# Weight conversions of the expert stage: all low parts on VectorE, weights in the long unit's first product, w-pieces in the second products

## The chip, the cores and the metric

The kernel runs on one core of a Trainium2 chip. The metric is the device time of one launch in microseconds (us). TensorE's clock has two levels, 1.2 and 2.4 GHz; the profile shows the granted clock of a stretch as a share of full speed.

## What is computed

Local attention over chunks feeds a mixture of eight experts (two per token), and that feeds a dense block with a maximum over three products. All of it is float32. The expert stage, where the change lies, is the middle function:

```python
def _moe_ref(x, w_gate, w_noise, noise, w1, w2):      # x 3072x512, w1 8x512x1024, w2 8x1024x512
    ...
    top2 = np.argpartition(-noisy_logits, 2, axis=1)[:, :2]
    ...
    for e in range(E):
        for k in range(2):
            mask = top2[:, k] == e
            h = np.maximum(x[mask] @ w1[e], 0.0)
            out[mask] += top2_w[mask, k, None] * (h @ w2[e])

def _moe2_ref(x, w1, w2, w3, w_out):                   # w1, w2, w3 512x768, w_out 768x512
    h = np.maximum(np.maximum(x @ w1, x @ w2), x @ w3)
    return h @ w_out
```

## The kernel before

**Precision.** A float32 product is made of three matrix products of a reduced type (`three`): high x high, high x low, low x high. So each operand is kept in two tiles, `hi` and `lo`. `split` makes them: ScalarE copies the source into `hi` (a cast), and then another engine subtracts, `lo = src - hi`. That engine is GpSimd (the page's POOL) unless the caller names VectorE (DVE).

**Expert stage.** It runs in 16 units, two per expert: an even, long unit (four token tiles of 128, 512 rows; unit 0 has 384) and an odd, short one (320 rows: two tiles and 64; unit 1 has 448). `unit(u)` has two parts. The **first product** has 8 steps; each makes 12 matmuls into one of two PSUM banks, `sc` and `pp` in turn, then ScalarE's relu writes `h[:, 0]` (L788) and VectorE writes the low part `h[:, 1]` from the same bank (L792). TensorE may overwrite a bank two steps later, after both have read it. The **second product** has 8 steps for each token tile (steps 8 to 39 in a long unit, 8 to 31 in a short one), sums into one of three banks (`misc`, `tabp`, `po`), and `put` copies each finished tile out, in turn by ScalarE (L656) and VectorE (L658). `unit_turn` transposes a token tile of the next unit and splits it into `xT`, its low part on VectorE, four times per second product (the last at step 28 of a long unit).

**Side tasks.** Two kinds of work are hung on the steps by a table, `planned(u)`: at each step the tasks are issued behind the relu and the low part of that step. The program's order is the code's order, on every engine, and each engine runs its own instructions in that order.

- A **weight tile**: 128x1024 floats of w1 or w2 (eight per expert). `wload` loads it on SyncE's queue into one of three staging buffers `st`; `wsplit` casts it on ScalarE (L195), subtracts on GpSimd (L196), then loads the part that stands three places further on. There are 12 tile slots.
- A **w-piece**: 24 parts of the later dense block's weights, which arrive as 64-bit numbers. `narrow` makes float32 of one in five VectorE instructions (L241 to L245) behind a square on ScalarE, and adds on GpSimd (L246). For the 18 pieces of the first three weight matrices `sums` forms four differences on VectorE (L204) and `cast` splits the eight blocks, with ScalarE (L195) and GpSimd (L196), and stores both parts to DRAM (`m2s`). The other six are only stored (`m2f`).

In the table of before, a long unit of experts 1 to 6 has four pieces, at steps 1, 4, 12 and 26 (`sums` at 3, 6, 20, 34 and `cast` at 4, 7, 22, 36), and six weight tiles at 0, 3, 9, 16, 24 and 32; a short unit has two weight tiles, at 9 and 14. The six pieces that are only stored come last, in units 10 and 12. So units 2, 4, 6, 8 and 10 have differences and casts in their first product, and units 2, 4, 6 and 8 have them at the end of the second one.

**Dense block.** Block 0 (`second`, four token tiles) makes 18 products of 12 matmuls, the calls of `step(s)` standing ahead of product s. In it the rows of block 1 are gathered (`block_fetch`, GpSimd's queue), weighted (`block_mix`, L690 and L691 on VectorE) at even s and transposed (`block_turn`, L703 on TensorE) at odd s.

Of the kernel before, what the change touches and what calls it, by code (L numbers as in the profile page):

```python
# [8 lines left out]
F32 = mybir.dt.float32  # L9
F32R = mybir.dt.float32r  # L10
# [40 lines left out]
def tile_kernel(ctx, tc, qT, kT, mkT, vw, wgn, noise, w1, w2, m2w, out):  # L51
# [103 lines left out]
    turns = [("f64", j, h) for j in range(12) for h in range(2)]  # L155
    wparts, plan = list(range(8)), []

    def planned(u):

        e = u // 2  # L160
        if u == 0:
            return [(8 + k, None) for k in range(4)]
        if u % 2:
            return [(8 * e + 12 + k, 9 + 5 * k) for k in range(2)]
        c = [(turns.pop(0), *at) for at in ((1, 3, 4), (4, 6, 7), (12, 20, 22), (26, 34, 36)) if turns]
        w = [(8 * e + 6, 0), (8 * e + 7, 3), (8 * e + 8, 9), (8 * e + 9, 16), (8 * e + 10, 24), (8 * e + 11, 32)]
        return sorted(c + w, key=lambda x: x[1])

    for u in range(2 * E):
        plan.append([x for x in planned(u) if not isinstance(x[0], int) or x[0] < 8 * E])  # L170
        wparts += [x[0] for x in plan[u]]
# [28 lines left out]
    def sums():  # L200

        for v, j, h in formed[-1:]:
            for o, l, r, op in ((0, 7, 6, ALU.add), (1, 0, 4, ALU.subtract), (2, 4, 7, ALU.subtract), (3, 5, 1, ALU.subtract)):
                DVE.tensor_tensor(v[:, o, :], v[:, l, :], v[:, r, :], op=op)  # L204

    def cast():

        while formed:
            v, j, h = formed.pop()
            top = made["cv"].tile([128, 8, 128], F32R, name="top", bufs=1)  # L210
            split(v, top, v.bitcast(F32R))
            for r, t in enumerate((top, v)):
                SP.dma_start(m2s[j, :, :, h, r, :].rearrange("o p n -> p o n"), t if r else t.bitcast(F32))

    def wsplit(eng=None):
        n = wnext[1]
        if n == len(wparts):
            return
        wnext[1] += 1
        st = wst.pop(n)  # L220
        if isinstance(wparts[n], int):
            w = wtile(wparts[n])
            split(st, w[:, 0, :], w[:, 1, :], eng)
        else:
            _, j, h = wparts[n]
            val = narrow(st.rearrange("p (n t) -> p n t", t=2))
            if j < 9:
                formed.append((val, j, h))
            else:
                SP.dma_start(m2f[j - 9, :, 512 * h:512 * h + 512], val[:, 4:8, :].rearrange("p i n -> p (i n)"))  # L230
        wload()

    def narrow(st):
# [6 lines left out]
        ACT.activation(sq, top.bitcast(F32), AF.Square)  # L240
        DVE.tensor_scalar(val, top, 5, 2, op0=ALU.logical_shift_left, op1=ALU.logical_shift_right)  # L241
        DVE.scalar_tensor_tensor(val, top, -(1 << 30), val, op0=ALU.bitwise_and, op1=ALU.bitwise_or)
        DVE.scalar_tensor_tensor(v, sq, 2.0 ** -30, v, op0=ALU.is_ge, op1=ALU.mult)
        DVE.tensor_scalar(top, val, -(1 << 23), None, op0=ALU.bitwise_and)
        DVE.scalar_tensor_tensor(sq, low.bitcast(U32), 2.0 ** -52, top.bitcast(F32), op0=ALU.mult, op1=ALU.mult)  # L245
        POOL.tensor_tensor(v, v, sq, op=ALU.add)  # L246
        return full
# [518 lines left out]

    def unit(u):
# [5 lines left out]
        else:  # L773
            side = [[] for _ in range(steps)]
            for _, *at in plan[u]:
                for i, task in zip(at, (wsplit, sums, cast)):
                    side[i].append(task)
# [77 lines left out]
    def second(xT, dst, step=lambda s: None, along=[]):  # L855
# [275 lines left out]
```

## Time and profile before

| | |
|---|---|
| median of 3 runs | 1181.28 us (1180.49 to 1181.43) |
| profiled execution, its own time | 1179.27 us |
| its span | 1177.5 us |
| TensorE matmuls (PE) busy | 1121.1 us, 95% of the span |
| VectorE (DVE) busy | 592.2 us, 50% |
| GpSimd (POOL) busy | 416.1 us, 35% |
| ScalarE (ACT) busy | 390.2 us, 33% |

The busy time of one engine is an average over stages with different limits, and a busy TensorE is not TensorE at its peak. The stages are better read by stretches: how long a unit takes, and at which granted clock. The units' borders are the starts of their first matmuls into `sc` in the timeline.

### The profile page before, as it was taken

To read this page: it belongs to the slowest core of one execution; us is meant where nothing else is said; L and a number is where in the kernel's file an instruction comes from. 1 tells how busy PE (TensorE), PEld (TensorE's weight loads), DVE (VectorE), ACT (ScalarE), POOL (GpSimd) and SP (SyncE) were. 2 spreads that over 40 slices of the span, in tenths; PEclk is the share of its full clock that TensorE was granted. 3 is DMA by queue.
4 is the path that set the end of the run, shared out by engine and by line. 5 is a ranking of instruction groups with operands and counts; after the bars stand their busy time and mean duration, and the time that the engine had idled before them with its cause. 6 is when DMAs were issued, how large, how long until landed. Compare 5 with 4: busy or idle time off the path is not lost. (4 is left out here: it accounts for less than half of the span.)

```text
span 1177.5 us, 17436 instructions
## 1 busy us (share of the span) xinstructions
PE 1121.1 (95%) x6804; PEld 935.5 (79%) x6804; DVE 592.2 (50%) x1164; ACT 390.2 (33%) x680; POOL 416.1 (35%) x331
## 2 busy tenths in 40 slices
PE   8887999999999999999999999999999999999997
PEld 5777878878788778788788898887787778787886
DVE  4587862463563662572633422135566675655221
ACT  5877422332332332333323322222321143113110
POOL 3001021355354363463444432133266524543000
PEclk9999799999999999999999999999999999999999
DMA  8999551365465374473553546257466744766501
GB/s 239 309 292 287 164 170 34 120 195 170 146 191 190 114 222 141 130 237 112 161 180 125 154 160 188 72 153 227 141 185 217 230 129 134 223 188 214 179 1 39
DMA packets 113690, 199.07 MB, mean 169 GB/s; under 512 B 8576, under 2 KB 46592, under 8 KB 113600
## 3 DMA queue, kind: packets, MB, share of 16 engines
q1 hardware_dynamic: 76736, 109.86, 29.8%
q0 software_dynamic: 34272, 78.13, 21.5%
q10 hardware_dynamic: 2592, 9.88, 2.6%
q8 instruction: 56, 0.92, 0.3%
q14 instruction: 34, 0.28, 0.1%
HBM read 151.18 MB, written 46.66 MB: 168 GB/s over the span
## 5 line engine op out<-in xcount | busy, mean ns | idle before, releaser
L93 PE MATMUL pp<-xT,w 128*128 128x512 f32 (+3 forms) x912 | 199.6, 369 | 12.9 <-DVE h L792 12.9
L93 PE MATMUL sc<-xT,w 128*128 128x512 f32 (+3 forms) x912 | 195.0, 361 | 8.7 <-DVE h L792 7.3
L93 PEld LDWEIGHTS pp<-xT,w 128*128 128x128 f32 x912 | 163.9, 196 | 36.4 <-DVE h L792 15.4
L93 PEld LDWEIGHTS sc<-xT,w 128*128 128x128 f32 x912 | 158.2, 190 | 33.7 <-ACT h L788 8.2
L196 POOL TENSOR_TENSOR w<-st,w 128x1024 fp32r<-128x1024 f32 x52 | 126.9, 2442 | 149.1 <-ACT w L195 149.1
L93 PE MATMUL po<-w,h 128*128 128x512 f32 x548 | 135.1, 395 | 0.0
L93 PE MATMUL misc<-w,h 128*128 128x512 f32 x522 | 127.8, 394 | 0.0
L93 PE MATMUL tabp<-w,h 128*128 128x512 f32 x498 | 121.5, 394 | 0.0
L93 PEld LDWEIGHTS po<-w,h 128*128 128x128 f32 x548 | 101.0, 188 | 20.6
L93 PEld LDWEIGHTS misc<-w,h 128*128 128x128 f32 x522 | 96.5, 188 | 19.8
L93 PEld LDWEIGHTS tabp<-w,h 128*128 128x128 f32 x498 | 92.2, 188 | 19.0
L252 POOL DMA_INDIRECT g<-xd,tok x56 | 53.2, 949 | 107.8 <-DVE count_i L535 50.0
L792 DVE SCALAR_TENSOR_TENSOR h<-sc,h 128x256 fp32r<-128x256 f32 (+2 forms) x96 | 39.7, 442 | 84.9 <-ACT h L788 84.9
L792 DVE SCALAR_TENSOR_TENSOR h<-pp,h 128x256 fp32r<-128x256 f32 (+2 forms) x96 | 39.8, 443 | 82.6 <-ACT h L788 82.6
L252 POOL DMA_INDIRECT g<-ys,rows x48 | 49.7, 1035 | 87.4 <-DMA ys<-y 46.1
L195 ACT CAST w<-st 128x1024 fp32r<-128x1024 f32 x75 | 78.3, 1046 | 3.2 <-DVE st L896 2.8
L788 ACT ACTIVATE h<-sc 128x512 fp32r<-128x512 f32 (+3 forms) x64 | 33.1, 517 | 111.5 <-PE sc L93 111.5
L788 ACT ACTIVATE h<-pp 128x512 fp32r<-128x512 f32 (+3 forms) x64 | 33.1, 517 | 108.8 <-PE pp L93 108.8
L196 POOL TENSOR_TENSOR val<-val,top 128x1024 fp32r<-128x1024 f32 x18 | 45.5, 2527 | 52.9 <-ACT top L195 52.9
L196 DVE TENSOR_TENSOR xT<-xp,xT 128x512 fp32r<-128x512 f32 (+1 forms) x35 | 23.4, 668 | 66.2 <-ACT xT L195 66.2
L246 POOL TENSOR_TENSOR val<-val,sq 128x512 f32<-128x512 f32 x24 | 30.9, 1287 | 65.4 <-DVE sq L245 62.2
L196 DVE TENSOR_TENSOR xT<-idle,xT 128x512 fp32r<-128x512 f32 (+1 forms) x29 | 18.7, 645 | 61.8 <-ACT xT L195 61.8
(196 smaller groups left out, 1649.4 us busy)
## 6 DMA issues: line engine op xcount, KB each, us to landing
st<-in_w SPq DMA_DIRECT2D x64, 512.0 KB, 3.6
w<-m2s POOLq DMA_DIRECT2D x27, 1024.0 KB, 9.1
ys<-y SPq DMA_DIRECT2D x48, 256.0 KB, 3.9
st<-in_m2w SPq DMA_DIRECT2D x24, 512.0 KB, 3.8
m2s<-top SPq DMA_DIRECT2D x18, 512.0 KB, 3.6
m2s<-val SPq DMA_DIRECT2D x18, 512.0 KB, 3.2
xT<-m2s POOLq DMA_DIRECT2D x9, 1024.0 KB, 5.9
w<-m2s POOLq DMA_DIRECT2D x9, 768.0 KB, 7.2
```

Source lines behind the costliest of these rows:

```text
L93: PE.matmul(o, l, r, start=start, stop=stop)
L195: ACT.copy(hi, src)
L196: (eng or POOL).tensor_tensor(lo, src, hi.bitcast(F32), op=ALU.subtract)
L246: POOL.tensor_tensor(v, v, sq, op=ALU.add)
L252: POOL.indirect_dma_start(out=g[0:n], out_offset=None, in_=src, in_offset=bass.IndirectOffsetOnAxis(ap=idx, axis=0))
L788: ACT.activation(h[:, 0, 0:n], p[:, 0:n], AF.Relu)
L792: DVE.scalar_tensor_tensor(o[:, c], p[:, c], 0.0, h[:, 0, c].bitcast(F32), op0=ALU.max, op1=ALU.subtract)
```

## The change

The table becomes another one. All eight weight tiles of a long unit (its own w2 and the next expert's w1) stand in its first product, the cast of tile k at step k and its subtraction at step k+1. Short units have none. A piece is cut in five tasks (`one` to `five`) at steps i, i+2, i+4, i+5 and i+6: i is 9 in a short unit, 9, 18 and 27 in the long units of experts 2, 4 and 6 (units 4, 8, 12), and 9 and 22 in the other long ones. The six pieces that are only stored come first. All subtractions and additions of both kinds go to VectorE; GpSimd keeps its DMA issues in this stage. The loads move with the tasks: after the subtraction of a weight tile, after `two` of a piece.

In block 0, transposes and gathers move from ahead of a product into its middle (`middle`, behind six of its 12 matmuls), and the last transpose one step later into the second product.

```diff
-    turns = [("f64", j, h) for j in range(12) for h in range(2)]
+    turns = [("f64", j, h) for j in (9, 10, 11, *range(9)) for h in range(2)]
...
         if u == 0:
-            return [(8 + k, None) for k in range(4)]
-        if u % 2:
-            return [(8 * e + 12 + k, 9 + 5 * k) for k in range(2)]
-        c = [(turns.pop(0), *at) for at in ((1, 3, 4), (4, 6, 7), (12, 20, 22), (26, 34, 36)) if turns]
-        w = [(8 * e + 6, 0), (8 * e + 7, 3), (8 * e + 8, 9), (8 * e + 9, 16), (8 * e + 10, 24), (8 * e + 11, 32)]
-        return sorted(c + w, key=lambda x: x[1])
+            return [(8 + k,) for k in range(4)]
+        w = [] if u % 2 else [(8 * e + 4 + k, k, k + 1) for k in range(8) if 8 * e + 4 + k < 8 * E]
+        at = [9] if u % 2 else [9, 18, 27] if e % 2 == 0 else [9, 22]
+        return w + [(turns.pop(0), i, i + 2, i + 4, i + 5, i + 6) for i in at if turns]
...
+            def low(eng):
+                (eng or POOL).tensor_tensor(w[:, 1, :], st, w[:, 0, :].bitcast(F32), op=ALU.subtract)
+                wload()
+
+            return [n, lambda eng: ACT.copy(w[:, 0, :], st), low]
...
-        POOL.tensor_tensor(v, v, sq, op=ALU.add)
-        return full
...
+        def one(eng):
+            ACT.activation(sq, top.bitcast(F32), AF.Square)
+            DVE.tensor_scalar(val, top, 5, 2, op0=ALU.logical_shift_left, op1=ALU.logical_shift_right)
+            DVE.scalar_tensor_tensor(val, top, -(1 << 30), val, op0=ALU.bitwise_and, op1=ALU.bitwise_or)
+
+        def two(eng):
+            DVE.scalar_tensor_tensor(v, sq, 2.0 ** -30, v, op0=ALU.is_ge, op1=ALU.mult)
+            DVE.tensor_scalar(top, val, -(1 << 23), None, op0=ALU.bitwise_and)
+            DVE.scalar_tensor_tensor(sq, low.bitcast(U32), 2.0 ** -52, top.bitcast(F32), op0=ALU.mult, op1=ALU.mult)
+            wload()
+
+        def three(eng):
+            DVE.tensor_tensor(v, v, sq, op=ALU.add)
+            if j >= 9:
+                SP.dma_start(m2f[j - 9, :, 512 * h:512 * h + 512], v)
+                return
+            for o, l, r, op in ((0, 7, 6, ALU.add), (1, 0, 4, ALU.subtract), (2, 4, 7, ALU.subtract), (3, 5, 1, ALU.subtract)):
+                DVE.tensor_tensor(full[:, o, :], full[:, l, :], full[:, r, :], op=op)
+
+        def four(eng):
+            if j < 9:
+                hi.append(made["cv"].tile([128, 8, 128], F32R, name="top", bufs=1))
+                ACT.copy(hi[0], full)
+
+        def five(eng):
+            if j < 9:
+                DVE.tensor_tensor(full.bitcast(F32R), full, hi[0].bitcast(F32), op=ALU.subtract)
+                for r, t in enumerate((hi[0].bitcast(F32), full)):
+                    SP.dma_start(m2s[j, :, :, h, r, :].rearrange("o p n -> p o n"), t)
...
                     for k in range(4):
+                        if k == 2:
+                            middle(6 * f + 2 * w + r)
...
-        side[3].insert(0, partial(step, 19))
+        side[4].insert(0, partial(middle, 19))
...
-            if s % 2 and s >= 5:
-                block_turn(b + 1, s // 2 - 2)
-                block_fetch(b + 1, s // 2)
...
+        def middle(s):
+            if s % 2 and s >= 5:
+                block_turn(b + 1, s // 2 - 2)
+                block_fetch(b + 1, s // 2)
```

Three places show what stands in a row now. The first is VectorE in the first product of unit 8 (a long unit); `h_2064` and those that follow are the eight `h` tiles, `val`, `sq` and `st` belong to the pieces, `w` is a weight tile. Before:

```order
L792 SCALAR_TENSOR_TENSOR h_2064<-sc,h_2064 128x512
L792 SCALAR_TENSOR_TENSOR h_2065<-pp,h_2065 128x512
L241 TENSOR_SCALAR val<-st 128x512
L242 SCALAR_TENSOR_TENSOR val<-st,val 128x512
L243 SCALAR_TENSOR_TENSOR val<-sq,val 128x512
L244 TENSOR_SCALAR st<-val 128x512
L245 SCALAR_TENSOR_TENSOR sq<-st 128x512
L792 SCALAR_TENSOR_TENSOR h_2066<-sc,h_2066 128x512
L792 SCALAR_TENSOR_TENSOR h_2067<-pp,h_2067 128x512
L204 TENSOR_TENSOR val<-val 128x128 x4
L792 SCALAR_TENSOR_TENSOR h_2068<-sc,h_2068 128x512
```

The same place now:

```order
L811 SCALAR_TENSOR_TENSOR h_2064<-sc,h_2064 128x512
L811 SCALAR_TENSOR_TENSOR h_2065<-pp,h_2065 128x512
L213 TENSOR_TENSOR w_122<-st,w_122 128x1024
L811 SCALAR_TENSOR_TENSOR h_2066<-sc,h_2066 128x512
L213 TENSOR_TENSOR w_123<-st,w_123 128x1024
L811 SCALAR_TENSOR_TENSOR h_2067<-pp,h_2067 128x512
L213 TENSOR_TENSOR w_124<-st,w_124 128x1024
L811 SCALAR_TENSOR_TENSOR h_2068<-sc,h_2068 128x512
```

The groups of four and five instructions between two `h` are gone; one weight subtraction stands in each gap instead.

The second place is VectorE at the end of unit 8, from its last piece to the first `h` of unit 9. Before:

```order
L241 TENSOR_SCALAR val<-st 128x512
L242 SCALAR_TENSOR_TENSOR val<-st,val 128x512
L243 SCALAR_TENSOR_TENSOR val<-sq,val 128x512
L244 TENSOR_SCALAR st<-val 128x512
L245 SCALAR_TENSOR_TENSOR sq<-st 128x512
L196 TENSOR_TENSOR xT_2063<-xp,xT_2063 128x4x64
L204 TENSOR_TENSOR val<-val 128x128 x4
L658 COPY y<-tabp 128x512
L792 SCALAR_TENSOR_TENSOR h_2064<-sc,h_2064 128x256
```

Now:

```order
L231 TENSOR_SCALAR val<-st 128x512
L232 SCALAR_TENSOR_TENSOR val<-st,val 128x512
L194 TENSOR_TENSOR xT_2063<-xp,xT_2063 128x4x64
L235 SCALAR_TENSOR_TENSOR val<-sq,val 128x512
L236 TENSOR_SCALAR st<-val 128x512
L237 SCALAR_TENSOR_TENSOR sq<-st 128x512
L241 TENSOR_TENSOR val<-val,sq 128x512
L246 TENSOR_TENSOR val<-val 128x128 x4
L255 TENSOR_TENSOR val<-val,top 128x1024
L670 COPY y<-tabp 128x512
L811 SCALAR_TENSOR_TENSOR h_2064<-sc,h_2064 128x256
```

The addition (L241) and the piece's subtraction (L255) have come to VectorE, ahead of the copy of `y` and the next unit's first `h`.

The third place is TensorE in block 0, at two of its products; `xp` is the bank of the transposes. Before:

```order
L93 MATMUL sc<-xT_130,w_6646 128x512 x12
L703 MATMUL xp<-ident,g 128x128 x4
L93 MATMUL pp<-xT_130,w_6646 128x512 x12
L93 MATMUL idle<-xT_130,w_6722 128x512 x12
L703 MATMUL xp<-ident,g 128x128 x4
```

Now:

```order
L93 MATMUL sc<-xT_130,w_6646 128x512 x12
L93 MATMUL pp<-xT_130,w_6646 128x512 x6
L715 MATMUL xp<-ident,g 128x128 x4
L93 MATMUL pp<-xT_130,w_6646 128x512 x6
L93 MATMUL idle<-xT_130,w_6722 128x512 x12
L93 MATMUL sc<-xT_130,w_6722 128x512 x6
L715 MATMUL xp<-ident,g 128x128 x4
```

The four transposes stand half a product further on.

## Rows read from the trace of the kernel before

**Rows 1.** Windows: stretch, length, engines' busy us (instructions), granted clock, DMA share, GB/s.
```profile
217.70:267.20 49.50, 46.88 (x205) 37.83 (x204) 32.94 (x46) 18.84 (x27) 25.31 (x13) 0.97 0.51 156
267.20:301.40 34.20, 32.39 (x178) 29.13 (x176) 11.06 (x26) 9.15 (x16) 16.12 (x11) 0.95 0.58 183
301.40:351.60 50.20, 47.32 (x205) 37.95 (x205) 33.31 (x46) 18.86 (x27) 25.30 (x13) 0.97 0.51 155
351.60:384.20 32.60, 30.82 (x177) 27.54 (x177) 11.00 (x26) 9.15 (x16) 16.12 (x11) 1.00 0.58 190
...
632.20:678.00 45.80, 45.57 (x206) 36.91 (x206) 20.44 (x34) 16.12 (x24) 19.95 (x11) 1.00 0.44 133
678.00:708.50 30.50, 30.50 (x177) 27.51 (x176) 7.99 (x22) 8.32 (x15) 10.87 (x9) 1.00 0.44 155
```

**Rows 2.** Timeline, unit 2's first product: start us, us, engine, instruction [idle <- releaser].
```profile
234.54 2.69 POOL L196 TENSOR_TENSOR val<-val,top 128x1024 fp32r<-128x1024 f32 x1 [1.57 <-ACT top L195]
235.09 2.70 DVE L243 SCALAR_TENSOR_TENSOR val<-sq,val 128x512 f32<-128x512 f32 x1
239.63 4.38 PE L93 MATMUL pp<-xT,w 128*128 128x512 f32 x12 [2.62 <-DVE h L792]
```

**Rows 3.** Timeline, start of unit 3.
```profile
267.22 3.22 DVE L204 TENSOR_TENSOR val<-val 128x128 f32<-128x128 f32 x4 [1.06 <-POOL val L246]
270.60 1.04 ACT L195 CAST top<-val 128x1024 fp32r<-128x1024 f32 x1 [7.08 <-DVE val L204]
272.71 3.02 PE L93 MATMUL sc<-xT,w 128*128 128x320 f32 x12 [1.81 <-DVE h L792]
```

**Rows 4.** Timeline, first product of unit 14 (no wait in it).
```profile
717.21 2.88 PE L93 MATMUL pp<-xT,w 128*128 128x512 f32 x12
717.47 0.60 ACT L788 ACTIVATE h<-sc 128x512 fp32r<-128x512 f32 x1 [2.12 <-PE sc L93]
718.10 0.69 DVE L792 SCALAR_TENSOR_TENSOR h<-sc,h 128x512 fp32r<-128x512 f32 x1 [2.02 <-ACT h L788]
719.93 2.88 PE L93 MATMUL sc<-xT,w 128*128 128x512 f32 x12
```

**Rows 5.** Instructions of tile w on VectorE: ns min/median/max, first and last start.
```profile
L196 DVE TENSOR_TENSOR w<-st,w x23: 1210/1224/2231, 112.7 to 982.1; 128x1024 fp32r<-128x1024 f32 x23
```

**Rows 6.** Loads into st, units 2 to 14: us from issue to landing.
```profile
DMA to landing us min/median/max: 3.5/3.8/4.9
```

**Rows 7.** Timeline, VectorE in a piece of unit 2: its first, last instruction, its differences.
```profile
224.66 0.42 DVE L241 TENSOR_SCALAR val<-st 128x512 int32<-128x512 int32 x1
...
227.17 0.69 DVE L245 SCALAR_TENSOR_TENSOR sq<-st 128x512 f32<-128x512 uint32 x1
...
240.36 1.02 DVE L204 TENSOR_TENSOR val<-val 128x128 f32<-128x128 f32 x4 [0.19 <-POOL val L246]
```

**Rows 8.** Line 243, all 24 executions: ns min/median/max, first and last start.
```profile
L243 DVE SCALAR_TENSOR_TENSOR val<-sq,val x24: 691/693/2700, 225.9 to 671.7; 128x512 f32<-128x512 f32 x24
```

**Rows 9.** Timeline, second product of unit 12 and first steps of unit 13.
```profile
654.61 3.56 PE L93 MATMUL misc<-w,h 128*128 128x512 f32 x15
...
677.98 1.92 PE L93 MATMUL sc<-xT,w 128*128 128x320 f32 x12
678.18 0.69 DVE L658 COPY y<-misc 128x512 f32<-128x512 f32 x1 [4.24 <-PE misc L93]
...
680.46 0.56 DVE L792 SCALAR_TENSOR_TENSOR h<-sc,h 128x256 fp32r<-128x256 f32 x2 [1.59 <-ACT h L788]
...
681.49 0.75 PE L93 MATMUL sc<-xT,w 128*128 128x320 f32 x4
```

**Rows 10.** The page's costliest groups: busy us, mean ns | idle before, releaser.
```profile
L196 DVE TENSOR_TENSOR xT<-xp,xT 128x512 fp32r<-128x512 f32 (+1 forms) x35 | 23.4, 668 | 66.2 <-ACT xT L195 66.2
```

**Rows 11.** Waits of TensorE in block 0: us in total, times, longest.
```profile
PE xp L703 <- DVE g L691: 2.2, 2, 1.4
PE xp L703 <- ACT h L870: 0.7, 1, 0.7
```

More of the change, by code (lines that the diff above doesn't have):

```diff
@@ L161, in planned @@
         if u == 0:
-            return [(8 + k, None) for k in range(4)]
-        if u % 2:
-            return [(8 * e + 12 + k, 9 + 5 * k) for k in range(2)]
-        c = [(turns.pop(0), *at) for at in ((1, 3, 4), (4, 6, 7), (12, 20, 22), (26, 34, 36)) if turns]
-        w = [(8 * e + 6, 0), (8 * e + 7, 3), (8 * e + 8, 9), (8 * e + 9, 16), (8 * e + 10, 24), (8 * e + 11, 32)]
-        return sorted(c + w, key=lambda x: x[1])
+            return [(8 + k,) for k in range(4)]
+        w = [] if u % 2 else [(8 * e + 4 + k, k, k + 1) for k in range(8) if 8 * e + 4 + k < 8 * E]
+        at = [9] if u % 2 else [9, 18, 27] if e % 2 == 0 else [9, 22]
+        return w + [(turns.pop(0), i, i + 2, i + 4, i + 5, i + 6) for i in at if turns]
     for u in range(2 * E):
-        plan.append([x for x in planned(u) if not isinstance(x[0], int) or x[0] < 8 * E])
+        plan.append(planned(u))
         wparts += [x[0] for x in plan[u]]
@@ L198, in tile_kernel, with wtasks @@
     formed = []
[L200 to L213, printed above, removed]
     def wsplit(eng=None):
+        for task in wtasks()[1:]:
+            task(eng)
+    def wtasks():
         n = wnext[1]
         if n == len(wparts):
-            return
+            return [n]
         wnext[1] += 1
@@ L222, in wsplit, with narrow @@
             w = wtile(wparts[n])
[L223 to L233, printed above, removed]
+            def low(eng):
+                (eng or POOL).tensor_tensor(w[:, 1, :], st, w[:, 0, :].bitcast(F32), op=ALU.subtract)
+                wload()
+            return [n, lambda eng: ACT.copy(w[:, 0, :], st), low]
+        _, j, h = wparts[n]
+        return [n] + narrow(st.rearrange("p (n t) -> p n t", t=2), j, h)
+    def narrow(st, j, h):
         top, low = st[:, :, 1], st[:, :, 0]
@@ L239, in narrow @@
         sq = made["cv"].tile([128, 512], F32, name="sq", bufs=1)
[L240 to L245, printed above, removed]
-        POOL.tensor_tensor(v, v, sq, op=ALU.add)
-        return full
+        hi = []
+        def one(eng):
[23 more added lines that the diff above has]
+                    SP.dma_start(m2s[j, :, :, h, r, :].rearrange("o p n -> p o n"), t)
+        return [one, two, three, four, five]
     def fetch(src, idx, n):
@@ L765, in ahead, with task_of @@
                     task(0, j)
+    def task_of(part, now, i):
+        if i == 0:
+            now += wtasks()
+            assert wparts[now.pop(0)] == part
+        now[i](DVE)
     def unit(u):
@@ L774, in unit @@
             side = [[] for _ in range(steps)]
-            for _, *at in plan[u]:
-                for i, task in zip(at, (wsplit, sums, cast)):
-                    side[i].append(task)
+            for part, *at in plan[u]:
+                now = []
+                for i, t in enumerate(at):
+                    side[t].append(partial(task_of, part, now, i))
         for f in range(8):
@@ L853, in out_part, with second @@
         three(o, h, w, i == 0, i == 5)
-    def second(xT, dst, step=lambda s: None, along=[]):
+    def second(xT, dst, step=lambda s: None, middle=lambda s: None, along=[]):
         h = [big.tile([128, 2, 512], F32R, name=f"h{i}") for i in range(6)]
@@ L1024, in block @@
                     block_fetch(1, j)
-            second(xTs["b", b] if b else xts[0], dst, step, along)
+            second(xTs["b", b] if b else xts[0], dst, step, middle, along)
     for b in range(len(blocks)):
```

## The prediction

> **What bounds the kernel now.** I read the windows first, one for each unit of the expert stage. Unit 12, a long one, takes 45.8 us and unit 13, a short one, 30.5, both at a granted clock of 1.00 and with matmuls over practically the whole window. Unit 2 takes 49.5 and unit 4 50.2; units 6, 8 and 10 are like unit 4 (50.2 to 50.3). Unit 3 takes 34.2 at a clock of 0.95 and unit 5 32.6 at 1.00; unit 7 is like unit 3, unit 9 like unit 5 [rows 1]. The same matmuls run in all long units from unit 2 on, and the same in all short ones from unit 3 on, so nine units lose 2 to 4.5 us each and the rest of the stage loses next to nothing. TensorE is the bound, and those losses are what a side engine can give back.
>
> Then the timeline, inside such a unit. In unit 2 the low part of an `h`, on VectorE, comes late, TensorE waits 2.62 us for its bank, and the 12 matmuls behind the wait take 4.38 us [rows 2] where an undisturbed product starts the next one 2.72 later (719.93 - 717.21) [rows 4]: they run in part at the lower clock, 1.2 GHz instead of 2.4. Why is the low part late? Five instructions of a piece stand ahead of it, and one, L243, takes 2.70 us beside a GpSimd subtraction of 2.69 us that began just earlier [rows 2]; its usual time is 0.69 [rows 8]. At the start of unit 3 it goes through ScalarE: its cast of `top` waited for four differences that took 3.22 us, and the relu stands behind that cast; TensorE waits 1.81 us [rows 3]. Last I looked at block 0, where TensorE waits 2.9 us for transposes' operands and their bank [rows 11].
>
> **The change part by part.**
>
> *Removed: the piece work between two `h` of a long unit's first product, and casts of pieces at the end of its second product's GpSimd chain.* If the nine units fall to the undisturbed length, the long ones give 49.5 + 4 x 50.2 - 5 x 45.8 = 21.3 us, and the short ones 2 x 34.2 + 2 x 32.6 - 4 x 30.5 = 11.6 us [rows 1]. Together 32.9; the cost of the lower clock is in these lengths and isn't added again.
>
> *Added in the first product: eight subtractions and eight casts of weight tiles.* One subtraction on VectorE is 1.22 us [rows 5], one `h` 0.69 [rows 4], so 1.91 us of the 2.72 of a step. Does it delay an `h`? Product sc ends when pp begins, at 717.21; relu runs from 717.47, `h` from 718.10 to 718.79, and its bank is wanted at 719.93 [rows 4], 1.1 us later. The next `h` can start 2.72 us after this one; the subtraction between them ends 1.91 after it. So no wait. ScalarE has 0.60 + about 1.05 (the cast of the same size in [rows 3]) of 2.72. I cost this part at nothing, under the cover of TensorE's own step, and that cover has an end: see the loads below.
>
> *Added in second products: pieces, wholly on VectorE.* A piece's first five instructions take 227.17 + 0.69 - 224.66 = 3.20 us; the addition 0.69 (by the row of the same size in [rows 8]) and the differences 1.02 [rows 7] make 1.76 with a hand-over; ScalarE's cast 1.04 [rows 3] and two hand-overs 1.15; the last subtraction 1.22 [rows 5], 1.27 with one. This is one chain of 7.4 us, since each task needs the one before it and VectorE runs in order. In a short unit it is one chain, in a long one with two it ends long before the unit. Units 8 and 12 have three full ones (unit 4 has two of the short, stored kind). From the start of the second product: the last `h` is done at about 1.6, two weight subtractions bring 4.0, three chains 26.2, three `xT` low parts on the way (0.67 each [rows 10], the last a half tile) 28.0, the copy of `y` 0.69 [rows 9] 28.7, the next unit's first `h` 0.56 [rows 9] 29.2. TensorE wants that bank at 681.49 - 654.61 = 26.9 [rows 9]. So the `h` is late by 2.4 us in units 9 and 13. The other end: with the bare durations (2.92 for the five, 0.4 less over each chain) it is late by 1.2. I take 2.4, since the 3.20 is a measured sequence. Of the short units' waits of about 1.8 us two of four came with the lower clock, at 1.6 us more (34.2 against 32.6) [rows 1]; half of that on each makes 3.2. Two units: **6.4 us** lost, between 2.4 and 8.0.
>
> With two full pieces the same count is 4.0 + 14.8 + 1.8 + 0.7 (the copy that no longer falls into a gap) = 21.3, then the `y` copy at the unit's end and `h` behind its relu, before 26.9: nothing lost.
>
> *GpSimd* loses its arithmetic in the stage. What it keeps (gathers and the loads of `m2s`) can issue earlier, and nobody waits for it: the units without a wait had the same gathers. I cost it at nothing either way. SyncE's queue carries the same loads and stores in another order; behind a load that waits for a subtraction stand the stores of `y`, which have three buffers.
>
> At this point a rule bears on which durations hold. L243 took 2.70 us beside GpSimd and 0.69 else [rows 2, 8]. The Trainium skill, SBUF — State Buffer, section "Who interferes with whom", says that VectorE and GpSimd share one pair of ports as an exclusive lock, and that a VectorE instruction with two SBUF inputs is blocked for the whole of a GpSimd instruction that reads SBUF. The trace agrees: 2.70 is the 0.69 and the rest of the 2.69. By that rule the short durations hold once GpSimd does no arithmetic there; without it, the second rival's time would stand.
>
> *Block 0.* Half a product is 1.36 us, so the waits of 1.4 and 0.7 us ahead of transposes vanish; the last transpose moves three matmuls, 0.68, against 0.7. Of 2.9 us [rows 11] I take **2.8**; at the least 2, if what is late moves along.
>
> **Sum.** 1179.27 (profiled execution: span 1177.5 and 1.77 around it) - 32.9 - 2.8 + 6.4 = 1150.0. The profiled execution is 2.0 below the median of the runs, so the median to expect is **1152.0**, 2.5% faster.
>
> **The rivals.**
>
> 1. *No tail.* VectorE ends its three chains in time, because the hand-overs are hidden or the first piece starts before the last weight tile's step. For it: the 1.2 us of the lower end need little more to vanish. Against: the order puts the pieces behind both subtractions and ahead of the next `h`. 1179.27 - 32.9 - 2.8 + 2.0 = 1145.6.
>
> 2. *Stretched pieces.* VectorE's instructions are long for another reason than GpSimd, and L243's 2.70 or the differences' 3.22 come back: about 2.2 us more in each chain. With two pieces the tail ends 21.3 + 4.4 + 0.7 + 0.6 = 27.0 against 26.9, just on time; with three, 6.6 us later still. 1152.0 + 2 x 6.6 = 1165. For it: the maxima in rows 5 and 8. Against: each that I looked at lay beside a GpSimd instruction.
>
> 3. *Loads set the pace, slower than before.* There are three staging buffers. The load of tile k+3 starts when the subtraction of tile k is done; its landing, cast (1.05), the relu behind it (0.6), the `h` (0.69 and a hand-over) and the subtraction (1.22) make landing + 3.6 us for three steps of 2.72. At the median landing of 3.8 us [rows 6] that is 7.4 of 8.2 us; 4.6 us is where it begins to bind, and the 1.1 us of slack of a bank hold it to about 5.7. Loads are denser now: eight behind one first product instead of four. If they took 8 us, the cast in front of a relu would be 3.5 us late by the sixth tile and 7 by the eighth, less the slack 5.9, with 1.6 for the clock 7.5 in each of the six units with eight tiles: 45 us on the 1145.6, 1190. It outweighs the gain from a landing of about 7.3 us on. Against: 4.9 is the longest seen.
>
> 4. *The wait only changes its place.* The late `h` comes from something beside the pieces and stays: 1181. Against: units 12 and 13, with the same `h` and no differences, lose nothing.
>
> **How the numbers follow.** The forecast has 0.56 (1147 to 1157 by the bounds of the tails), no tail 0.24, stretched pieces or tails in more units 0.13, slow loads 0.04, no change of use 0.03. The range 1144 to 1161 holds the first two and part of the third. A measurement of this kernel can tell some 0.2% (2.4 us) from no change. Slower by more: 0.04, the loads. Within it: 0.03. Faster: 0.93.
>
> **What would show it.** Right: units 2, 4, 6, 8 and 10 at 45 to 46 us and units 3, 5 and 7 at 30.5, at a clock of 1.00; in units 9 and 13 one wait of TensorE for `h`, near their third product, of 1 to 3 us; L235, the old L243, never above 0.75 us; the weight subtraction near 1.22 in all units; no ScalarE wait for `st` above 2 us; block 0 some 3 us shorter. Wrong: ScalarE's casts of `w` waiting for DMA in long units (the third rival), a wait for `h` in the first product of a long unit, or piece chains well above 7.4 us.

## The result and the profile after

The changed kernel takes 1148.47 us (median of 4 runs, 1147.20 to 1151.13), the kernel before 1181.36 beside it: a ratio of 0.9725 with an interval of 0.9704 to 0.9745. The profiled execution took 1149.49 us, with a span of 1147.7. So the change makes the kernel 2.75% faster; 1152.0 was predicted, with a range of 1144 to 1161, so the time lies inside it, 3.5 us under the forecast.

The windows of the changed kernel, in the columns of [rows 1]: units 4 and 5, unit 9, unit 13, unit 14, and block 0.

```profile
295.00:340.70 45.70, 45.47 (x206) 37.10 (x206) 30.77 (x45) 18.89 (x26) 3.27 (x4) 1.00 0.58 186
340.70:371.20 30.50, 30.50 (x177) 27.51 (x176) 13.57 (x33) 7.83 (x15) 3.27 (x4) 1.00 0.42 126
493.20:525.20 32.00, 30.80 (x178) 27.57 (x176) 15.76 (x39) 8.78 (x16) 3.32 (x4) 1.00 0.53 152
647.10:679.30 32.20, 30.82 (x177) 27.55 (x177) 15.96 (x39) 8.79 (x16) 5.04 (x6) 1.00 0.49 150
679.30:726.50 47.20, 45.80 (x206) 37.05 (x206) 24.35 (x39) 15.33 (x23) 0.81 (x2) 1.00 0.72 223
757.50:822.00 64.50, 64.49 (x300) 53.04 (x299) 33.59 (x45) 19.75 (x29) 24.48 (x24) 1.00 0.59 176
```

Unit 4 was 50.2 us at a clock of 0.97 and unit 5 was 32.6 [rows 1]; they are 45.7 and 30.5 now, with matmuls over the whole window and a clock of 1.00. Units 2 to 8 and 10 are all like this (45.2 to 45.7 and 30.5 to 30.6). GpSimd is busy for 3.3 us in unit 4 instead of 25.3; over the whole span it falls from 416.1 to 215.9 us, and VectorE, which took the arithmetic over, only rises from 592.2 to 632.7. Three units are longer than their kind: 9 and 13 (32.0 and 32.2 where 30.5 is undisturbed), and 14 (47.2 where it took 45.7 before).

All waits of TensorE for `h` between unit 2 and the end of unit 15 are one group of the waits (us in total, times, longest):

```profile
PE sc L93 <- DVE h L811: 3.8, 3, 1.4
```

In the kernel before, nine units had one each, of 2.62 us in [rows 2] and 1.81 in [rows 3]. The three that are left are the three long windows above. Line 243 is now L235, and its durations in all 24 executions, with those of the weight subtraction, can be set beside [rows 8] and [rows 5] (ns, min/median/max):

```profile
L235 DVE SCALAR_TENSOR_TENSOR val<-sq,val x24: 681/682/694, 199.9 to 715.6; 128x512 f32<-128x512 f32 x24
...
L213 DVE TENSOR_TENSOR w<-st,w x67: 1212/1215/1241, 114.7 to 782.0; 128x1024 fp32r<-128x1024 f32 x67
```

The longest of line 243 was 2700 ns; the longest L235 is 694. No weight subtraction by L213 is above 1241 ns. The 2231 of [rows 5] is no counterpart: it ran in the dense block (857.38 us), where subtractions of this size still take up to 2586 ns in the changed kernel.

Stage by stage, predicted and measured:

| stage | predicted, us | measured, us |
|---|---|---|
| units 2 to 10, without the wait in unit 9 | -32.9 | 351.7 - 1.4 - 383.9 = -33.6 |
| late `h` in units 9 and 13 | +6.4 | 1.4 + 1.7 = +3.1 |
| unit 14 | 0 | 47.2 - 45.7 = +1.5 |
| from the end of unit 15 to the start of the last block | -2.8 | 317.5 - 320.6 = -3.1 |
| ahead of unit 2, and the last stretch | 0 | +1.5 and +1.0 |
| sum | -29.3 | -29.6 |

The two spans differ by 29.8; the 0.2 that is left is 0.1 in each of units 11 and 12, the precision of the windows. The change hardly touches the two stretches of the line before the sum (it puts one piece into unit 1, which takes 41.4 us in both kernels): the stage ahead of unit 0 took 132.8 us before and 134.0 after, and between 130.2 and 137.2 in the profiled executions of this study. So the length of a unit is a sharper measure than a median here.

### The profile page after: what moved, and what is told of

Read it like the earlier page. It is cut to its first block, busy times and chain, and to the rows that moved or that the text cites. A ratio compares the mean times of both kernels' runs of the same rounds, so it can differ in the third digit from the quotient of the medians.

```text
span 1147.7 us, 17323 instructions
## 1 busy us (share of the span) xinstructions
PE 1106.3 (96%) x6803; PEld 927.2 (81%) x6804; DVE 632.7 (55%) x1258; ACT 391.6 (34%) x680; POOL 215.9 (19%) x237
## 5 line engine op out<-in xcount | busy, mean ns | idle before, releaser
L93 PE MATMUL pp<-xT,w 128*128 128x512 f32 (+3 forms) x912 | 190.5, 356 | 0.0
L93 PEld LDWEIGHTS pp<-xT,w 128*128 128x128 f32 x912 | 157.4, 188 | 19.5 <-DVE h L811 0.2
L213 DVE TENSOR_TENSOR w<-st,w 128x1024 fp32r<-128x1024 f32 x67 | 81.0, 1217 | 11.2 <-ACT w L216 11.0
L216 ACT CAST w<-st 128x1024 fp32r<-128x1024 f32 x67 | 70.1, 1046 | 4.4 <-DMA st<-in_w 4.0
L93 PE MATMUL po<-v,pt 128*32 128x130 f32 x768 | 30.1, 294 | 17.7 <-ACT pt L383 8.9
L251 ACT CAST top<-val 128x1024 fp32r<-128x1024 f32 x18 | 18.9, 1049 | 80.2 <-DVE val L246 68.3
L93 PEld LDWEIGHTS po<-v,pt 128*32 128x32 f32 x768 | 22.3, 115 | 24.2 <-ACT pt L383 12.6
```

The lines of the kernel that those rows point to most:

```text
L93: PE.matmul(o, l, r, start=start, stop=stop)
L213: (eng or POOL).tensor_tensor(w[:, 1, :], st, w[:, 0, :].bitcast(F32), op=ALU.subtract)
L216: return [n, lambda eng: ACT.copy(w[:, 0, :], st), low]
L251: ACT.copy(hi[0], full)
```

## The experiments

The theory is that of the prediction: the piece work stood between two `h` on VectorE, GpSimd's arithmetic stretched it, TensorE waited for the bank. Two causes are mixed in it (the place of the pieces and the engine of the arithmetic), so the first pair takes them apart. The others ask about the three units that got longer, about the place of the weights, the loads and block 0.

### The new places, arithmetic back on GpSimd

```diff
         def three(eng):
-            DVE.tensor_tensor(v, v, sq, op=ALU.add)
+            POOL.tensor_tensor(v, v, sq, op=ALU.add)
...
             if j < 9:
-                DVE.tensor_tensor(full.bitcast(F32R), full, hi[0].bitcast(F32), op=ALU.subtract)
+                POOL.tensor_tensor(full.bitcast(F32R), full, hi[0].bitcast(F32), op=ALU.subtract)
...
-        now[i](DVE)
+        now[i](None)
```

> The changed kernel with the weight tiles' and pieces' subtractions and the pieces' addition of units 1 to 15 put back on GpSimd: the new places without the new engine. Theory (the place is what counts: piece work between two h of a long unit's first product made the h late): long units stay at 45.7 us and short ones at 30.6 at a granted clock of 1.00, the tails of units 9 and 13 vanish because a piece's last subtraction no longer stands ahead of the next h on VectorE; median 1146 to 1150. In its second products single VectorE instructions of pieces still last 2 to 3 us beside a GpSimd subtraction, at no cost. Rival (GpSimd's arithmetic is what counts, because it stretches VectorE's instructions): units of 47 to 50 us, waits of TensorE for h, median 1160 or more.

Measured: 1150.08 us (1145.64 to 1150.46), ratio 0.9734 with 0.9706 to 0.9762. That is the changed kernel's time: the new places alone bring all of it. Long units take 45.7 us and short ones 30.6 (units 4 and 5):

```profile
294.20:339.90 45.70, 45.47 (x205) 37.11 (x205) 21.70 (x33) 18.68 (x26) 24.18 (x12) 1.00 0.50 160
339.90:370.50 30.60, 30.60 (x177) 27.57 (x177) 11.76 (x31) 7.83 (x15) 11.55 (x10) 1.00 0.47 139
```

From unit 2 to the end of unit 15 this kernel is even 2.1 us shorter than the changed one (536.2 against 538.3): with the new places, arithmetic on VectorE brings nothing more, and unit 14 shows below what it costs. The stretching is still there, but it lies under slack. VectorE and GpSimd in the second product of unit 8 (timeline):

```profile
489.08 2.21 DVE L235 SCALAR_TENSOR_TENSOR val<-sq,val 128x512 f32<-128x512 f32 x1
...
487.95 2.79 POOL L255 TENSOR_TENSOR val<-val,top 128x1024 fp32r<-128x1024 f32 x1 [2.35 <-ACT top L251]
```

L235 takes 2.21 us beside a GpSimd subtraction, as L243 did in [rows 2], and nobody waits for it, because no `h` stands behind it. I had expected the late `h` of units 9 and 13 to vanish with the shorter chain on VectorE, and that was a miss: these units took 31.8 and 31.7. There the relu of the first `h` stands on ScalarE behind a cast of `top` (495.07 us), whose differences wait for GpSimd's addition. The tail went through another engine.

### The old table, arithmetic on VectorE

```diff
-        (eng or POOL).tensor_tensor(lo, src, hi.bitcast(F32), op=ALU.subtract)
+        (eng or DVE).tensor_tensor(lo, src, hi.bitcast(F32), op=ALU.subtract)
...
-        POOL.tensor_tensor(v, v, sq, op=ALU.add)
+        DVE.tensor_tensor(v, v, sq, op=ALU.add)
```

> The kernel before with all subtractions and the addition on VectorE, table of places unchanged: the new engine without the new places. Theory (the place counts): L243 never above 0.75 us, yet units 2, 4, 6, 8 and 10 still wait for h, since five instructions and the addition, 3.9 us, stand between two h, and a cast of 1.05 and a subtraction of 1.22 us besides where a weight tile's task stands: long units of 48 to 52 us at a clock below 1.00; median 1168 to 1186. Rival (GpSimd's arithmetic counts): the stretching is gone and so are the waits, long units at 46, median 1150 to 1156.

Measured: 1167.68 us (1166.86 to 1169.83), ratio 0.9887 with 0.9857 to 0.9917, just under the expected 1168. The engine alone is worth 13.9 us, well under half. Its windows of units 4, 5 and 6, and its first product of unit 4 (timeline):

```profile
299.00:347.60 48.60, 46.07 (x206) 36.96 (x205) 37.15 (x63) 19.76 (x28) 3.45 (x4) 1.00 0.64 199
347.60:378.20 30.60, 30.60 (x178) 27.60 (x176) 11.65 (x25) 8.59 (x16) 3.34 (x4) 1.00 0.42 139
378.20:428.40 50.20, 47.67 (x205) 38.05 (x205) 37.09 (x63) 19.47 (x28) 3.65 (x4) 0.97 0.60 184
```

```profile
315.72 1.23 DVE L196 TENSOR_TENSOR val<-val,top 128x1024 fp32r<-128x1024 f32 x1 [0.25 <-ACT top L195]
...
316.86 0.42 DVE L241 TENSOR_SCALAR val<-st 128x512 int32<-128x512 int32 x1
...
320.03 0.69 DVE L246 TENSOR_TENSOR val<-val,sq 128x512 f32<-128x512 f32 x1
320.64 0.68 DVE L792 SCALAR_TENSOR_TENSOR h<-pp,h 128x512 fp32r<-128x512 f32 x1
...
321.37 1.89 PE L93 MATMUL pp<-xT,w 128*128 128x512 f32 x7 [1.88 <-DVE h L792]
```

The short units are clean: 30.6 us where [rows 1] has 34.2 and 32.6, which is 11.2 us over four of them. All that they lost came from GpSimd's slow links in the chain of [rows 3]. The long units keep most of their loss. No instruction of the piece is stretched (line 243 is 691 to 695 ns in all 24 executions), but seven of them in a row, from 315.72 to 320.64, still take 4.9 us between two `h`, against a step of 2.72. Units 6 and 10, with the lower clock of 0.97 besides, are as long as before, and unit 12, which lost nothing before, takes 47.1. Place and engine overlap: 31.5 us for the one alone, 13.9 for the other, 32.9 for both, where the first and the last hold the 3.1 us of block 0 as well.

### One piece of each long unit back in the first product

```diff
-        return w + [(turns.pop(0), i, i + 2, i + 4, i + 5, i + 6) for i in at if turns]
+        c = [(turns.pop(0), i, i + 2, i + 4, i + 5, i + 6) for i in at if turns]
+        if w and c and e < 7:
+            return w[:1] + [(c[0][0], 1, 1, 3, 4, 5)] + w[1:] + c[1:]
+        return w + c
```

> The changed kernel with one piece of each of units 2 to 12 (long ones) moved from step 9 to steps 1, 1, 3, 4 and 5 of the first product, still all on VectorE. Theory (place): a subtraction of 1.22 and five instructions of 3.2 us stand between two h, 4.4 us against the 2.0 that are free and 1.1 of slack, so TensorE waits about 1.3 us in each of the six units (47 us, with the lower clock 48.6), less in unit 2 to 4 no less; the tails of units 9 and 13 vanish (-2.9); median 1152 to 1164. Rival (GpSimd): no wait, no tail, median 1145 to 1147.

Measured: 1156.90 us (1155.63 to 1160.41), ratio 0.9796 with 0.9764 to 0.9828. Nothing else changes, no arithmetic of the loop is on GpSimd, and the wait is back. First product of unit 4 (timeline):

```profile
307.49 0.42 DVE L234 TENSOR_SCALAR val<-st 128x512 int32<-128x512 int32 x1
...
310.54 0.68 DVE L814 SCALAR_TENSOR_TENSOR h<-sc,h 128x512 fp32r<-128x512 f32 x1
...
311.28 0.98 PE L93 MATMUL sc<-xT,w 128*128 128x512 f32 x3 [0.82 <-DVE h L814]
```

Five instructions, from 307.49 to 310.54, stand between two `h` besides the weight subtraction that is there in the changed kernel too (306.36, 1.22 us). TensorE waits 0.82 us, in each of the six units; 1.3 was expected. Long units take 46.4 to 47.2 us, and units 9 and 13 are 30.6, since a piece less lies in the second products ahead of them. Here the place is the only cause.

### The weights spread as before, the pieces in the second products

```diff
-        w = [] if u % 2 else [(8 * e + 4 + k, k, k + 1) for k in range(8) if 8 * e + 4 + k < 8 * E]
+        s = [12, 16] if u % 2 else [0, 3, 12, 16, 22, 32] if e % 2 == 0 else [0, 3, 13, 17, 25, 32]
+        w = [((8 * e + 12 if u % 2 else 8 * e + 6) + k, i, i + 1) for k, i in enumerate(s)]
+        w = [x for x in w if x[0] < 8 * E]
...
-        return w + [(turns.pop(0), i, i + 2, i + 4, i + 5, i + 6) for i in at if turns]
+        return sorted(w + [(turns.pop(0), i, i + 2, i + 4, i + 5, i + 6) for i in at if turns], key=lambda x: x[1])
```

> The changed kernel with the weight tiles spread over all units about as before (six in a long unit at steps 0, 3, 12 or 13, 16 or 17, 22 or 25, 32, two in a short one at 12 and 16) and the pieces in the second products as changed, all on VectorE. Theory (the pieces' move out of the first product is what counts, the weights' place is a matter of room on VectorE in second products): units 2, 4, 6, 8, 10 and 12 at 45.7 us, units 3, 7 and 11 at 30.6; behind the three-piece units 8 and 12 VectorE ends 2 to 3 us later than in the changed kernel, units 9 and 13 at 33.5 to 36.5 us; 1151 to 1158 in all. Rival (the weights had to go into the first product for the gain): long units of 47 us or more.

One run: 1148.78 us, below the expected 1151 to 1158. But in this execution the stage ahead of unit 0, which the edit leaves alone, took 130.2 us, 3.8 less than in the changed kernel's, so the units are compared. Long units are 45.7, short ones 30.5, and unit 14 is 45.7 again. The one place where it loses is unit 9 (and 13, at 35.3); units 4 and 9:

```profile
290.70:336.40 45.70, 45.47 (x206) 37.10 (x206) 28.03 (x43) 16.83 (x24) 3.89 (x4) 1.00 0.47 148
488.80:524.00 35.20, 32.35 (x178) 29.12 (x176) 19.35 (x42) 11.51 (x19) 3.60 (x4) 0.95 0.57 172
```

So the gain hangs on the pieces' move. Putting all weight tiles in the first product matters for the room that it leaves on VectorE in the second one: with a weight subtraction in the way (492.87, 1.22 us) and a piece's load that VectorE waits for (0.91 us at 485.24), the tail's wait is 2.9 us, the clock falls to 0.95, and the unit takes 4.7 us more than 30.5, as expected (33.5 to 36.5). Against the changed kernel units 9 and 13 lose 6.3 us and unit 14 gains 1.5.

### The third pieces moved, and the load of unit 14 done earlier

Units 9, 13 and 14 are the price of the change. This edit takes the third full piece out of units 8 and 12, and converts the first weight tile of unit 14 in unit 13, so that the last load of weights is there before unit 14.

```diff
-        at = [9] if u % 2 else [9, 18, 27] if e % 2 == 0 else [9, 22]
-        return w + [(turns.pop(0), i, i + 2, i + 4, i + 5, i + 6) for i in at if turns]
+        if u == 14:
+            w = [(61 + k, k, k + 1) for k in range(3)]
+        at = [9] if u % 2 else [9, 18, 27] if e in (2, 7) else [9, 22]
+        return w + [(turns.pop(0), i, i + 2, i + 4, i + 5, i + 6) for i in at if turns] + [(60, 20, 21)] * (u == 13)
```

> The changed kernel with the third full piece of units 8 and 12 moved to units 14 and 15, and the first weight tile of unit 14 converted in unit 13 (steps 20 and 21). Theory: units 9 and 13 lose 1.4 and 1.6 us because three chains end behind their first h, and unit 14 loses 1.4 us because a cast of ScalarE waits for a load that shares the DMA engines with GpSimd's four large loads; all three fall to the undisturbed 30.6, 30.6 and 45.7, some 4.3 us, median 1143 to 1146. Rivals: the wait in unit 14 goes on to another load or unit (gain 2.9), or the three-piece unit 14 makes a tail of its own in unit 15 (31.0 becomes 32 or more).

Measured: 1146.20 us (1144.93 to 1150.51), ratio 0.9697 with 0.9672 to 0.9721, just above the expected 1143 to 1146. Units 9, 13 and 14 take 30.6, 30.6 and 45.7, as expected. But the pieces that were pushed back reach unit 15, which has `block_mix` on VectorE, and there one stands in the way: TensorE waits 2.57 us for `g`, the clock is 0.95 and the unit takes 35.4 instead of 31.0. The second version has the third pieces in units 2, 4 and 14 and none in 15:

```diff
-        at = [9] if u % 2 else [9, 18, 27] if e in (2, 7) else [9, 22]
+        at = ([9] if u < 15 else []) if u % 2 else [9, 18, 27] if e in (1, 2, 7) else [9, 22]
```

> The changed kernel with the third full piece of units 8 and 12 moved into units 2 and 14 (unit 2 then has three of the short, stored kind), none in unit 15, and the first weight tile of unit 14 converted in unit 13. Theory: units 9 and 13 fall to 30.6, unit 14 to 45.7, unit 15 stays at 31.0, since there VectorE's weighting of block 1's rows is again without a piece ahead of it (a piece there cost 4.4 us before); 4.3 us less than the changed kernel, median 1142 to 1146. Rival (the loss in unit 15 came from the third piece of unit 14, not from the piece in unit 15): unit 15 at 33 or more.

Measured: 1146.61 us (1142.67 to 1148.31), ratio 0.9706 with 0.9683 to 0.9730, a little above the expected 1142 to 1146. No wait of TensorE for an `h` is left between unit 2 and the end of unit 15. To set it beside the changed kernel, both ran once more on one chip.

> The changed kernel once more, on the chip on which the next run is timed: 1146 to 1151, a granted clock of 1.00 in all units, waits of 1 to 2 us in units 9, 13 and 14.

> The spread pieces once more, beside the changed kernel. Theory: its 4.3 us in units 9, 13 and 14 show in the median as well, 2 to 6 us below the changed kernel's; the attention stage ahead, whose length differed by up to 4 us between profiled executions, hides part of it. Rival: what the units gain comes back elsewhere, medians within 1 us.

The changed kernel took 1149.88 us (1147.87 to 1152.86, ratio 0.9730), this one 1145.75 (1144.89 to 1148.49, ratio 0.9698): 4.1 us less. The ratios' intervals overlap a little, but the windows say where it is; units 9, 13, 14 and 15 of this kernel:

```profile
496.20:526.70 30.50, 30.50 (x177) 27.50 (x176) 13.54 (x33) 7.83 (x15) 3.25 (x4) 1.00 0.34 105
648.70:679.20 30.50, 30.50 (x177) 27.51 (x176) 14.69 (x34) 8.78 (x16) 5.04 (x6) 1.00 0.35 101
679.20:724.90 45.70, 45.47 (x205) 37.10 (x205) 27.66 (x48) 15.86 (x24) 0.80 (x2) 1.00 0.75 237
724.90:755.90 31.00, 30.77 (x177) 27.49 (x176) 13.13 (x29) 7.80 (x16) 9.35 (x10) 1.00 0.66 194
```

Against the changed kernel these are 1.5, 1.7 and 1.5 us less, and nothing in unit 15: 4.7 together. By its units it is the best version of the study.

### GpSimd made busy in the first product

This kernel adds work whose result nobody uses: a memset and eight subtractions of 128x1024 on GpSimd, in the first products of the long units 2 to 12. They write and read the buffer that `top` has in the second products.

```diff
+            if u % 2 == 0 and 2 <= u <= 12:
+                if f == 0:
+                    idler = made["cv"].tile([128, 8, 128], F32, name="top", bufs=1)
+                    POOL.memset(idler, 0.0)
+                POOL.tensor_tensor(idler, idler, idler, op=ALU.subtract)
```

> The changed kernel with a subtraction of 128x1024 on GpSimd, on a tile that nobody uses, added at each of the eight steps of the first product of units 2 to 12 (and one memset a unit): it shares no data with VectorE. Theory (GpSimd reading SBUF blocks VectorE's instructions with two SBUF inputs for as long as it lasts): the weight subtractions on VectorE go from 1.22 to between 2 and 3.6 us, TensorE waits for h in each of these units, which grow from 45.7 to 49 to 54 us; in all 1170 to 1195. Rival (VectorE's long instructions had another cause): 1.22 us and 45.7 as before.

One run: 1152.38 us, far from the expected 1170 to 1195. GpSimd and VectorE in the first product of unit 8 (timeline), and the unit's window:

```profile
448.53 18.30 POOL L817 TENSOR_TENSOR top<-top 128x1024 f32<-128x1024 f32 x8
...
459.33 0.68 DVE L811 SCALAR_TENSOR_TENSOR h<-sc,h 128x512 fp32r<-128x512 f32 x1
459.93 2.31 DVE L213 TENSOR_TENSOR w<-st,w 128x1024 fp32r<-128x1024 f32 x1
462.16 0.68 DVE L811 SCALAR_TENSOR_TENSOR h<-pp,h 128x512 fp32r<-128x512 f32 x1
...
468.43 1.21 DVE L213 TENSOR_TENSOR w<-st,w 128x1024 fp32r<-128x1024 f32 x1
```

```profile
449.40:495.00 45.60, 45.37 (x205) 37.05 (x205) 36.45 (x49) 19.13 (x27) 21.63 (x12) 1.00 0.64 197
```

While GpSimd computes (448.53 to 466.83), a weight subtraction on VectorE takes 2.31 to 2.59 us; the first behind that takes 1.21. The two work on different tiles, so it is the engines that disturb each other. The Trainium skill, SBUF — State Buffer, section "Who interferes with whom", has it so for VectorE instructions with two SBUF inputs beside GpSimd instructions that read SBUF; the trace agrees, with 2.31 against 1.21. Both sides pay: the GpSimd subtraction that was running when the one of 459.93 began ended at 461.16, and VectorE's ended 1.08 us later; GpSimd's own take 2.76 us where one overlaps and 1.90 else. The `h` beside them, with one of its two inputs in PSUM, stays at 0.68. My price for it was wrong: I had expected 49 to 54 us for such a unit, and it takes 45.6. An `h` and a stretched subtraction take 462.16 - 459.33 = 2.83 us, 0.11 over a step; the first, with 2.59, is 0.40 over. Four such steps make the last `h` 0.74 us late, less than the 1.1 us that it may be, and then GpSimd is done.

### Two staging buffers instead of three

```diff
-    stage = ctx.enter_context(tc.tile_pool(name="stage", bufs=3))
+    stage = ctx.enter_context(tc.tile_pool(name="stage", bufs=2))
...
-            for _ in range(3):
+            for _ in range(2):
                 wload()
```

> The changed kernel with two staging buffers instead of three (two loads ahead). Theory (landing + 3.6 us is one turn of the buffers): with two, a turn of 7.4 us stands against two steps, 5.4; three turns make 5.9 us less 1.1 of slack, 4.8, with the lower clock 6.4: long units of experts 1 to 6 at 50.5 to 52 us, 1177 to 1190 in all. Rival (loads were no near thing, the buffers are not in the loop): long units within 1 us of 45.7.

One run: 1188.61 us, slower than the kernel before. ScalarE in the first product of unit 4 (timeline):

```profile
314.51 1.05 ACT L216 CAST w<-st 128x1024 fp32r<-128x1024 f32 x1 [2.85 <-DMA st<-in_w]
...
321.55 1.05 ACT L216 CAST w<-st 128x1024 fp32r<-128x1024 f32 x1 [2.82 <-DMA st<-in_w]
```

One turn of the buffers takes 321.55 - 314.51 = 7.04 us; the prediction's sum for it (landing + 3.6) gave 7.4. Two steps are only 5.44, so the loads set the pace. The long units 2 to 12 take 47.4 to 49.4 us; 50.5 to 52 was expected. In unit 4 (48.0) the miss is that only two of the three turns fall in the first product: the third turn's cast begins at 328.55, when TensorE is in the second product (from 326.73), so that it waits for two turns alone, 0.43 and 1.25 us. This is the third rival brought about on purpose: with a buffer less, it outweighs the whole gain. Of the 39.1 us that the span is longer, 18.1 are in these six units; units 9 and 13 lose another 9.5 and unit 14 loses 5.3.

### Block 0 as before

The calls of `middle` stand ahead of the product again.

```diff
+                    middle(6 * f + 2 * w + r)
                     step(6 * f + 2 * w + r)
...
-                        if k == 2:
-                            middle(6 * f + 2 * w + r)
...
-        side[4].insert(0, partial(middle, 19))
+        side[3].insert(0, partial(middle, 19))
```

> The changed kernel with block 0 as before: transposes and gathers ahead of a product, the last transpose at its old step. Theory: TensorE waits 2.9 us for transposes again and the stretch from unit 15's end to the last block grows by 2.8 to 3.4 us (317.5 to 320.5). Rival (the waits vanish anyway, as GpSimd is free earlier for gathers): 317.5.

One run: 1151.90 us. From the end of unit 15 to the start of the last block it takes 320.6 us where the changed kernel takes 317.5, and the waits of [rows 11] are back word for word at their new lines:

```profile
PE xp L715 <- DVE g L703: 2.2, 2, 1.4
PE xp L715 <- ACT h L890: 0.7, 1, 0.7
```

In block 0 of the changed kernel TensorE has no such wait. The part is worth 3.1 us and is independent of the rest: with the old table and block 0 as it was, the second experiment has 320.6 too.

## Why the prediction came true, and where it was wrong

**What bounds it, and the 32.9 us: right.** TensorE bounds the stage; nine units fell to their undisturbed length, and the sum over them is 33.6. The old table with VectorE's arithmetic, and the piece put back, show both halves of the cause.

**Eight weight tiles in the first product at no cost: right, up to unit 12.** VectorE in the first product of unit 8 of the changed kernel (timeline):

```profile
467.98 0.69 DVE L811 SCALAR_TENSOR_TENSOR h<-sc,h 128x512 fp32r<-128x512 f32 x1 [0.90 <-ACT h L807]
468.59 1.22 DVE L213 TENSOR_TENSOR w<-st,w 128x1024 fp32r<-128x1024 f32 x1
470.70 0.69 DVE L811 SCALAR_TENSOR_TENSOR h<-pp,h 128x512 fp32r<-128x512 f32 x1 [0.90 <-ACT h L807]
```

An `h` every 2.72 us, one subtraction between, and VectorE idle for 0.90 us until the next relu. From unit 2 to unit 13 ScalarE waits for weight loads 0.4 us in all.

**The late `h` in units 9 and 13: the mechanism was right, its size was not.** VectorE from the second piece of unit 8 on, and TensorE at the start of unit 9 (timeline):

```profile
480.13 1.23 DVE L255 TENSOR_TENSOR val<-val,top 128x1024 fp32r<-128x1024 f32 x1 [1.17 <-ACT top L251]
481.27 0.42 DVE L231 TENSOR_SCALAR val<-st 128x512 int32<-128x512 int32 x1
...
488.27 1.23 DVE L255 TENSOR_TENSOR val<-val,top 128x1024 fp32r<-128x1024 f32 x1 [1.04 <-ACT top L251]
489.41 0.42 DVE L231 TENSOR_SCALAR val<-st 128x512 int32<-128x512 int32 x1
...
495.62 1.23 DVE L255 TENSOR_TENSOR val<-val,top 128x1024 fp32r<-128x1024 f32 x1 [1.16 <-ACT top L251]
496.76 0.68 DVE L670 COPY y<-tabp 128x512 f32<-128x512 f32 x1
497.37 0.54 DVE L811 SCALAR_TENSOR_TENSOR h<-sc,h 128x256 fp32r<-128x256 f32 x2
```

```profile
493.18 1.92 PE L93 MATMUL sc<-xT,w 128*128 128x320 f32 x12
494.93 1.92 PE L93 MATMUL pp<-xT,w 128*128 128x320 f32 x12
498.06 1.99 PE L93 MATMUL sc<-xT,w 128*128 128x320 f32 x12 [1.20 <-DVE h L811]
```

Three chains in a row, then the copy of `y`, then the `h`, as counted; it is done at 497.37 + 0.54 = 497.91, 28.1 us into the second product (469.81) and not 29.2. TensorE wanted the bank at 496.68 (two products of 1.75 behind 493.18), 26.9 as counted, and goes on at 498.06; the trace counts 1.20 us of that as waiting. The step that failed is "I take 2.4, since the 3.20 is a measured sequence". The first five instructions of the chain take less where another stands between them: from 481.27 they run to 484.81, 3.54 us with the low part of an `xT` inside, which takes up 0.60 of it, so 2.94, close to the 2.92 of the other end. And an instruction that needs nothing of the one ahead begins some 0.08 us before the end that the trace gives that one. Over all that makes 1.1 us, some 0.5 of it in the three chains and the rest in the `xT` parts, the two subtractions ahead and the copy; the lower end of 1.2 was the right one. The clock's share ("half of that on each", 0.8) did not come at all: both units stayed at 1.00. Where the wait was 2.57 or 2.9 us, in other versions, the clock was 0.95 in the unit's window; at about 1.8 us, in the kernel before, [rows 1] has both 0.95 and 1.00.

**GpSimd: "I cost it at nothing either way" was wrong by 1.5 us, in unit 14.** Without arithmetic, GpSimd reaches the loads of `m2s` earlier. First product of unit 14 of the changed kernel (timeline; the first row is the last of four such loads, the others were issued from 676.85 on):

```profile
680.00 0.74 POOL L759 DMA_DIRECT2D w<-m2s  x1 [0.63 <-DVE xT L194]
...
688.10 0.38 SPq L186 DMA_DIRECT2D st<-in_w  x1
...
695.22 1.05 ACT L216 CAST w<-st 128x1024 fp32r<-128x1024 f32 x1 [3.60 <-DMA st<-in_w]
696.17 0.59 ACT L807 ACTIVATE h<-sc 128x512 fp32r<-128x512 f32 x1
...
697.54 3.01 PE L93 MATMUL sc<-xT,w 128*128 128x512 f32 x12 [1.17 <-DVE h L811]
```

In the kernel before, the four loads of 1 MB were issued at 715.99, 7.5 us into its unit 14, behind a subtraction. Now they are under way when the last load of weights is issued at 688.10; that one lands at about 695.2, 7.1 us later, where [rows 6] has 4.9 at the most. The cast waits, the relu stands behind it, then the `h`, then TensorE. This is the chain of the third rival, and its bound of 5.7 us of landing is passed, but what slows the load is GpSimd's queue and not "denser" loads, as the rival had it. That "nobody waits for it" was true of those loads and not of what shares the way with them. Where the arithmetic stays on GpSimd (the first experiment), the four loads are issued at 688.16, and unit 14 takes 45.7; with the weights spread as before, or their last load done early, it takes 45.7 too. The list of signs had this one, a wait of ScalarE for `st` above 2 us; the other that passed 2 us is 2.2, at the square of a piece, and nobody waited for that.

**Block 0: right**, 3.1 for 2.8.

**The sum was partly right by compensation.** The profiled execution was to take 1150.0 us and took 1149.49, but that is -0.7 in the units, -3.3 in the tails, +1.5 in unit 14, -0.3 in block 0 and +2.5 ahead of unit 2 and in the last stretch (the 0.2 of units 11 and 12 makes up the difference). That these all but cancel is luck. The last step, adding 2.0 for the median, did not carry over: this time the profiled execution is 1.0 above the median.

**The rivals.** No tail: the tails are there, half as large; the version without them, and without the loss in unit 14, came to 1145.75 and 1146.61 where the rival's sum gave 1145.6. Stretched pieces: no, 694 ns is the longest L235. Loads that set the pace: in one unit, by another cause, and in all the long ones from unit 2 on once a buffer is taken away. A wait that only changes its place: no.

## What to carry to other kernels

Side work in the order of an engine that frees a bank should fit, between two instructions that free one, into the slack of one step: seven short instructions in a row made TensorE wait 1.88 us here, where a row with a long one made it wait 2.62, and the same work in the second product, where no `h` stands behind it, costs nothing. Count its chain against the next point where that engine is wanted, and look for what stands on the other engines there. When an engine is relieved of work, ask which transfers it will issue earlier and what they will meet on the way.

## What the chip showed that I had not expected

- Independent instructions on VectorE begin before the end that the trace gives the one ahead: 0.69 us long and 0.61 apart (467.98 and 468.59), 1.23 long and 1.14 apart (480.13 and 481.27); of two that depend on each other, the second begins some 0.04 us behind that end (481.27 + 0.42 and 481.73).
- A load of 512 KB on SyncE's queue took 7.1 us to land beside four loads of 1 MB on GpSimd's queue, against a median of 3.8 in [rows 6].
- A subtraction on VectorE and one on GpSimd that overlap don't share the time: VectorE's took 2.31 us instead of 1.21 and GpSimd's 2.76 instead of 1.90. It cost the unit nothing (45.6 us), while five unstretched instructions of 3.05 us behind a subtraction of 1.22 made TensorE wait 0.82.
